# Reading q, k and V through one casting queue, and reordering the expert layer of a fused attention and mixture-of-experts kernel

## The chip, the cores and the metric

The kernel runs on one core of a Trainium2 chip. The core has five engines that work side by side: TensorE (PE: matrix products and transposes, with a separate row PEld for its weight loads), VectorE (DVE), ScalarE (ACT), GpSimd (POOL) and SyncE (SP). Sixteen DMA engines move data between DRAM and the core's memory. Three engines issue DMAs here: SP and ACT on hardware queues, POOL on a software queue (q0 in the profile) whose descriptors its own cores write, and which alone can cast f32 to bf16 on the way. The metric is the device time of one execution in microseconds (us); the median of several executions is compared.

## The reference

Block-causal attention over 8 batches, 8 heads, 576 positions and head size 64 is followed by a mixture of 8 experts on the 4,608 rows of 512 that attention yields. A row's expert is a hash of its token id.

```python
scores = scale * np.matmul(q, k.transpose(0, 1, 3, 2))     # (8, 8, 576, 576)
mask = (pos[:, None] // 64) >= (pos[None, :] // 64)
attn = softmax(np.where(mask, scores, -1e9))
x = np.matmul(attn, v).transpose(0, 2, 1, 3).reshape(4608, 512)
expert_idx = token_ids * 2654435761 % 8
for e in range(8):
    rows = expert_idx == e
    out[rows] = np.maximum(x[rows] @ w1[e], 0) @ w2[e]     # 512 -> 1024 -> 512
```

## The kernel before

The order of every engine's instructions is the order of the program text; each engine runs its own list strictly in that order and waits on semaphores where it needs another engine's result.

**Attention** is cut into 8 batches of four pairs (index g, 32 in all; r = g mod 4). A pair is two heads, one on partitions 0 to 63 and the other on 64 to 127. For each batch `load_qk` (L101) brings q and k as f32 on SP's queue, `cast_qk` (L109) casts them to bf16 on DVE, and `T_group` (L171) transposes 8 (or 4) blocks of 128x128 on PE into a PSUM tile `tp` and copies it into `qkT` with DVE (L184). Five T groups make a batch. `load_v` (L118) brings V as f32 in six DMAs on SP's queue, and `cast_v` (L152) casts it on POOL into the padded key tiles `vx` and `v4`, rows of 64 values and a 1 (so that the product also yields the row sums). There are two such sets.

For pair g the loop at L432 lays down, in this order: `S_chunk(g,0)` (scores of 512 queries, then an exponential on ACT, L220), one T group of the next batch (two when r = 3), `S_chunk(g,1)`, `PV(g-2,0)` (the product with V, L261), `S_chunk(g,2)` (with `S_rest` when r = 0), `PV(g-2,1)` and `norm(g-2)` on DVE (L271, L272). `scatter_x(b-1)` sends a finished batch's rows to a DRAM buffer sorted by expert, with five indirect DMAs on POOL's queue (L283). The slots come from `route`, some 40 small DVE instructions that are spread over the first pairs.

**The expert layer** begins once all rows are in DRAM. `load_x(e)` (L485) reads 640 rows of an expert on SP's queue, `turn_x(e)` (L505, L507) transposes them in groups of two 128-row tiles, through one PSUM buffer. `stage_a` (L520, 64 matmuls, relu on ACT) makes hT; `stage_b` (L535, 5 tiles of 8 matmuls) makes the output rows, which DVE copies (L540, four buffers `ysb`) and POOL scatters to DRAM (L542). `load_weights` (L398, L400) casts an expert's w1 and w2 through POOL's queue into three buffers. The main loop (L578) has, for each expert e: stage a, `turn_x(e+1)`, then `load_x(e+3)` and `load_weights(e+3)`, then stage b. Because `load_weights(e+3)` takes the buffers of expert e, POOL waits there until stage b of e has read w2, and the five scatters of e stand behind it on POOL.

Of the kernel before, what the change touches and what calls it, by code (L numbers as in the profile page):

```python
# [20 lines left out]
NT = 4  # L21
# [18 lines left out]
def kernel(  # L40
# [58 lines left out]
    qkf, qkb = {}, {}  # L99

    def load_qk(b, engs=(None, None)):  # L101
        for w, src in ((1, k), (0, q)):
            t = ld.tile([P, 2, JR, D], F32, name="qf" if w == 0 else "kf", tag="qf" if w == 0 else "kf")
            (engs[w] or nc.sync).dma_start(
                t[:].rearrange("p m j d -> p m (j d)"),
                src[b].rearrange("(m h) (g j) d -> (h g) m (j d)", m=2, j=JR))
            qkf[b, w] = t

    def cast_qk(b, w, j0=0, j1=JR, eng=None):  # L109
        if (b, w) not in qkb:  # L110
            qkb[b, w] = cst.tile([P, JR, 2, D], BF16, name="qb" if w == 0 else "kb",
                                 tag="qb" if w == 0 else "kb")
        o, i = qkb[b, w][:, j0:j1], qkf[b, w][:, :, j0:j1].rearrange("p m j d -> p j m d")
        (eng or nc.vector.tensor_copy)(o, i)

    vfs = {}

    def load_v(b):  # L118
        vf = lv.tile([P, 36, D], F32, name="vf", tag="vf")
        vm = vf[:, 0:32, :].rearrange("p (h i) d -> p h i d", h=H)  # L120
        for i in range(NT):
            nc.sync.dma_start(
                vm[:, :, i, :], v[b, :, 128 * i : 128 * i + 128, :].rearrange("h p d -> p h d"))
        for m in range(2):
            nc.sync.dma_start(
                vf[64 * m : 64 * m + 64, 32:36, :],
                v[b, 4 * m : 4 * m + 4, 512:576, :].rearrange("r s d -> s r d"))
        vfs[b] = vf

    vexts = []  # L130
    for z in range(2):
# [19 lines left out]

    def cast_v(b):  # L152
        vf = vfs.pop(b)
        vx, v4 = vexts[b % 2]
        nc.gpsimd.tensor_copy(  # L155
            vx[:, :, :, 0:D], vf[:, 0:32, :].rearrange("p (h i) d -> p h i d", h=H))
        for m in range(2):
            nc.gpsimd.tensor_copy(
                v4[64 * m : 64 * m + 64, :, m, 0:D], vf[64 * m : 64 * m + 64, 32:36, :])
# [6 lines left out]
        [(1, j) for j in range(16, 18)] + [(0, j) for j in range(16, 18)],  # L166
        [(1, j) for j in range(8, 16)],
        [(0, j) for j in range(8, 16)],
    )

    def T_group(b, n):  # L171
# [5 lines left out]
        for c, (w, j) in enumerate(items):  # L177
            nc.tensor.transpose(  # L178
                out=tp[:, c, :], in_=qkb[b, w][:, j].rearrange("p m d -> p (m d)"), identity=identbf[:])
        c = 0  # L180
        while c < len(items):
            w, j0 = items[c]
            n = sum(1 for x in items if x[0] == w)
            nc.vector.tensor_copy(  # L184
                qk[:, :, w, :].rearrange("p h (g j) -> p h g j", j=JR)[:, :, :, j0 : j0 + n],
                tp[:, c : c + n, :].rearrange("p j (h g) -> p h g j", h=NP))
            c += n
# [61 lines left out]
    def PV(g, m):  # L249
# [6 lines left out]
        vx, v4 = vexts[b % 2]  # L256
# [148 lines left out]
    load_qk(0, engs=(nc.scalar, None))  # L405
    load_v(0)
    load_qk(1)
    zx = const.tile([P, XW], BF16, name="zx")
    nc.gpsimd.memset(zx[:], 0.0)
    for e in range(E):  # L410
        nc.sync.dma_start(x_dram[(e + 1) * CAP - P : (e + 1) * CAP, :], zx[:])
    load_v(1)
# [11 lines left out]
    for n, (w, j0, j1) in enumerate(((1, 0, 8), (0, 0, 8), (1, 16, 18), (1, 8, 16), (0, 8, 16))):
        cast_qk(0, w, j0, j1)
        if n == 2:
            cast_qk(0, 0, 16, 18)
        T_group(0, n)
    cast_v(0)
    cast_qk(1, 1)  # L430
    cast_qk(1, 0)
    for g in range(NPAIRS + 2):  # L432
        b, r = divmod(g, NP)
        if g < NPAIRS:
            S_chunk(g, 0)
        if g + 1 < NPAIRS and b + 1 < B:
            T_group(b + 1, r)
            if r == 3:
                T_group(b + 1, 4)
# [13 lines left out]
        if r == 0 and b + 2 < B:  # L453
            load_qk(b + 2)
        if r == 1 and b + 2 < B:
            cast_qk(b + 2, 1)
        if r == 2 and b + 2 < B:
            cast_qk(b + 2, 0)
        if r == 1 and b >= 1:
            scatter_x(b - 1)  # L460
        if r == 2 and b + 1 < B:
            cast_v(b + 1)
            if b + 2 < B:
                load_v(b + 2)
        if g < NPAIRS:
            if b == 6 and r == 0:
                load_weights(0)
            if b == 7 and r == 0:
                load_weights(1)
            if b == 7 and r == 2:  # L470
                load_weights(2)
# [7 lines left out]
    psY = ffn_ctx.enter_context(tc.tile_pool(name="psY", bufs=3, space=PSUM))  # L479
    psX = ffn_ctx.enter_context(tc.tile_pool(name="psX", bufs=1, space=PSUM))  # L480
# [16 lines left out]
    def turn_x(e):  # L497
        xT = mx.tile([P, NKT, CAP], BF16, name="xT", tag="xT")
        xg = xgs[e]
        for g0 in range(0, G, 2):  # L500
            n = min(2, G - g0)
            tp = psX.tile([P, 2 * NKT, P], BF16, name="tx", tag="tx")
            for gg in range(n):
                for db in range(NKT):
                    nc.tensor.transpose(out=tp[:, gg * NKT + db, :],  # L505
                                        in_=xg[:, g0 + gg, db * P : (db + 1) * P], identity=identbf[:])
            nc.vector.tensor_copy(  # L507
                xT[:, :, g0 * P : (g0 + n) * P].rearrange("p d (g c) -> p g d c", g=n),
                tp[:, 0 : n * NKT, :].rearrange("p (g d) c -> p g d c", g=n))
        xTs[e] = xT  # L510
# [19 lines left out]
    def stage_b(e, hT):  # L530
        _, w2b = wtiles[e]
        for tt in range(G):
            yp = psY.tile([P, DM], F32, name="yp", tag="yp")
            for ft in range(NFT):
# [3 lines left out]
                )  # L538
            ysb = mo.tile([P, DM], F32, name="ysb", tag="ysb")
# [34 lines left out]
    for e in range(3):  # L574
        load_x(e)
    out_rows(0)
    turn_x(0)
# [178 lines left out]
```

## Time and profile before

| | |
|---|---|
| median of 3 runs | 376.84 us (372.2 to 377.64) |
| the profiled execution | 377.55 us; span 375.5 us from first to last instruction |
| busy share of the span | PE 74%, DVE 42%, ACT 39%, POOL 34% |
| mean granted TensorE clock | 0.89 of 2.4 GHz |
| DMA queues, share of 16 engines' time | q0 (POOL, software) 38.5%, 31.24 MB; q1 (SP) 31.6%, 33.86 MB; q10 (ACT) 0.9% |
| stretches (us from the span's start) | until the first score matmul 0 to 24.0; eight batches 24.0 to 136.5 (seven) and to 160.5; hand-over to the experts to 178.1; experts to 365.7; last scatters to 375.5 |

A row of the timeline is a start, a duration, the engine, the source line, the operation, output<-input, the shapes and a count; in brackets stands how long the engine had been idle and what ended that. DMA bytes are counted as written, so a cast to bf16 counts half of what it read.

### The profile page before, as it was taken

How to read it: one execution, taken by the hardware profiler on the slowest of the kernel's cores; microseconds unless marked ns; L12 is line 12 of the kernel's file. 1: busy time of each engine (PE TensorE's matmuls, PEld its weight loads, DVE VectorE, ACT ScalarE, POOL GpSimd, SP SyncE). 2: the span in 40 equal slices, each digit the busy share in tenths (PEclk: the TensorE clock that was granted, in tenths of full speed). 3: DMA queues.
4: the chain of work that ended last, by engine and by line, in shares of the span. 5: the costliest groups of instructions: out<-in, count | busy, mean ns of one | idle time of the engine just before them, and what ended most of it. 6: DMA issues, size and time to landing. Idle time of an engine off the chain costs nothing. (4 is left out here: it accounts for less than half of the span.)

```text
span 375.5 us, 6897 instructions
## 1 busy us (share of the span) xinstructions
PE 277.3 (74%) x2888; PEld 177.7 (47%) x2888; DVE 157.9 (42%) x278; ACT 144.8 (39%) x177; POOL 125.8 (34%) x155
## 2 busy tenths in 40 slices
PE   0358597897987867502989599598696895999990
PEld 0235465565665645402555446346254463464640
DVE  5679967877869533202031220220321312314230
ACT  1028497897887858100322304106014032050500
POOL 4303027547457645350003305104123151413241
PEclk9999898999989978555799979899699898999996
DMA  8999995979888788997266785778739756211121
GB/s 285 294 286 319 297 258 218 264 240 302 240 300 192 125 170 140 219 225 223 74 101 131 191 188 77 190 162 159 170 90 218 138 66 181 86 43 58 64 87 40
DMA packets 65971, 66.75 MB, mean 178 GB/s; under 512 B 39941, under 2 KB 54277, under 8 KB 65936
## 3 DMA queue, kind: packets, MB, share of 16 engines
q0 software_dynamic: 17536, 31.24, 38.5%
q1 hardware_dynamic: 48128, 33.86, 31.6%
q10 hardware_dynamic: 272, 1.18, 0.9%
q8 instruction: 23, 0.38, 0.4%
q14 instruction: 12, 0.10, 0.1%
HBM read 67.47 MB, written 16.61 MB: 224 GB/s over the span
## 5 line engine op out<-in xcount | busy, mean ns | idle before, releaser
L220 ACT ACTIVATE pt<-ps 128x1024 bf16<-128x1024 f32 x96 | 93.4, 1025 | 53.1 <-PE ps L203 39.8
L525 ACT ACTIVATE hT<-hp 128x640 bf16<-128x640 f32 x64 | 45.1, 704 | 158.5 <-PE hp L520 157.5
L535 PE MATMUL yp<-w2b,hT 128*128 128x512 bf16 x320 | 79.8, 414 | 0.0
L520 PE MATMUL hp<-xT,w1b 128*128 128x320 bf16 x512 | 73.7, 306 | 0.2 <-DVE xT L507 0.2
L540 DVE COPY ysb<-yp 128x512 f32<-128x512 f32 x40 | 27.7, 692 | 107.4 <-DMA out_dram<-ysb,perm 59.9
L542 POOL DMA_INDIRECT out_dram<-ysb,perm x40 | 40.0, 1000 | 69.7 <-DVE ysb L540 35.0
L520 PEld LDWEIGHTS <-w1b 128*128 128x128 bf16 x512 | 51.1, 100 | 22.6 <-issue 0.6
L283 POOL DMA_INDIRECT x_dram<-xs,slot_i x40 | 44.0, 1100 | 52.1 <-DVE xs L272 37.0
L194 PE MATMUL ps<-qkT 64*128 64x512 bf16 (+4 forms) x320 | 44.9, 328 | 16.8 <-DVE qkT L184 9.4
L535 PEld LDWEIGHTS <-hT 128*128 128x128 bf16 x320 | 33.5, 106 | 43.1 <-issue 12.6
L261 PE MATMUL O<-vx,pt 128*128 128x65 bf16 x896 | 44.3, 206 | 8.5 <-DVE xs L272 5.5
L184 DVE COPY qkT<-tp 128x1024 bf16<-128x1024 bf16 (+1 forms) x48 | 44.5, 950 | 9.0 <-PE tp L178 6.0
L505 PE MATMUL tx<-identbf,xg 128*128 128x128 bf16 x160 | 14.9, 240 | 41.7 <-DVE xT L507 26.9
L261 PEld LDWEIGHTS <-pt 128*128 128x128 bf16 x896 | 36.5, 105 | 14.2 <-DVE xs L272 4.4
L194 PEld LDWEIGHTS <-qkT 64*128 64x128 bf16 x320 | 18.3, 100 | 31.0 <-issue 12.1
L505 PEld LDWEIGHTS <-xg 128*128 128x128 bf16 x160 | 11.7, 107 | 44.5 <-issue 43.9
L507 DVE COPY xT<-tx 128x1024 bf16<-128x1024 bf16 (+1 forms) x24 | 14.4, 600 | 30.8 <-PE tx L505 30.8
L400 POOL DMA_DIRECT2D w2b<-in_moe_w_dram x8 | 7.6, 945 | 58.9 <-PE yp L535 58.9
L272 DVE TENSOR_TENSOR xs<-O,rsall 128x640 bf16<-128x640 f32 x32 | 26.4, 824 | 1.2
L203 PE MATMUL ps<-maskq,maskk 64*128 64x64 bf16 x256 | 25.0, 204 | 0.0
L155 POOL CAST vx<-vf 128x2048 bf16<-128x2048 f32 x8 | 15.2, 1902 | 21.4 <-DMA vf<-in_v_dram 21.4
L271 DVE RECIPROCAL rsall<-O 128x10 f32<-128x10 f32 x32 | 7.0, 218 | 34.3 <-PE O L264 23.0
(101 smaller groups left out, 160.5 us busy)
## 6 DMA issues: line engine op xcount, KB each, us to landing
kf<-in_k_dram SPq DMA_DIRECT2D x8, 1152.0 KB
vf<-in_v_dram SPq DMA_DIRECT2D x32, 256.0 KB
w1b<-in_moe_w_dram POOLq DMA_DIRECT2D x8, 1024.0 KB
w2b<-in_moe_w_dram POOLq DMA_DIRECT2D x8, 1024.0 KB
qf<-in_q_dram SPq DMA_DIRECT2D x7, 1152.0 KB
xg<-x_dram SPq DMA_DIRECT2D x8, 680.0 KB
qf<-in_q_dram ACTq DMA_DIRECT2D x1, 1152.0 KB
x_dram<-zx SPq DMA_DIRECT2D x8, 136.0 KB
```

The costliest lines, as they stand in the source:

```text
L184: nc.vector.tensor_copy(qk[:, :, w, :].rearrange("p h (g j) -> p h g j", j=JR)[:, :, :, j0 : j0 + n], tp[:, c : c + n, :].rearrange("p j ( ...
L194: nc.tensor.matmul(ps[:, m, o0 : o0 + n], lhsT=qk[rows, r, 1, 128 * i : 128 * i + 128], rhs=qk[rows, r, 0, q0 : q0 + n], start=True, stop= ...
L220: nc.scalar.activation(ptv[:, :, 512 * ch : 512 * ch + 512], ps[:], ACT.Exp, scale=SCALE)
L261: nc.tensor.matmul(dst, lhsT=pt[:, o0 : o0 + 128], rhs=vx[:, h, i, :], start=(i == 0), stop=(i == t))
L272: nc.vector.tensor_tensor(out=xss[b % 2][:, :, 0:DM].rearrange("p t (m r d) -> p m t r d", m=2, r=NP)[:, :, :, r, :], in0=Ov[:, :, :, 0:D] ...
L283: ins = nc.gpsimd.indirect_dma_start(out=x_dram[:, :], out_offset=bass.IndirectOffsetOnAxis(ap=slot_i[0:n, i, b : b + 1], axis=0), in_=xs[ ...
L505: nc.tensor.transpose(out=tp[:, gg * NKT + db, :], in_=xg[:, g0 + gg, db * P : (db + 1) * P], identity=identbf[:])
L520: nc.tensor.matmul(hp[:, t, 0:HC], lhsT=w1b[:, db, ft * P : (ft + 1) * P], rhs=xT[:, db, t * HC : (t + 1) * HC], start=(db == 0), stop=(db ...
L525: nc.scalar.activation(hT[:, ft, :].rearrange("p (t n) -> p t n", t=2), hp[:, :, 0:HC], ACT.Relu)
L535: nc.tensor.matmul(yp[:], lhsT=hT[:, ft, tt * P : (tt + 1) * P], rhs=w2b[:, ft, :], start=(ft == 0), stop=(ft == NFT - 1),)
L540: nc.vector.tensor_copy(ysb[:], yp[:])
L542: ins = nc.gpsimd.indirect_dma_start(out=out[:, :], out_offset=bass.IndirectOffsetOnAxis(ap=perm3[:, gg : gg + 1], axis=0), in_=ysb[:], in ...
```

## The change

It has five parts.

1. q, k and V are read by POOL's queue, which casts them on the way: `load_qk` writes bf16 `[P, 2, 18*64]` tiles in three buffers, `load_v` writes straight into three sets of `vx`/`v4`. The casts on DVE and POOL go, and so do the f32 tiles. Batch 0 of q and k comes in two halves. The constant fills (`set_fixed`) move from POOL to DVE.
2. The q and k tiles now keep the two head halves apart, so a block is transposed in two matmuls of 64 columns each, one per half (twice as many transposes).
3. The T groups of the next batch stand at other places: two at r = 0, two at r = 1, one at r = 2, none at r = 3. In batch 0 two of the five copies go to ACT.
4. In the expert layer `turn_x` works on one 128-row tile at a time, with two PSUM buffers, and tile tt of expert e+1 is turned inside stage b of e, behind tile tt's matmuls.
5. `load_x` and `load_weights` are issued two experts ahead, before stage a, and not three ahead, before stage b. Weights 0 and 1 are issued in attention, weights 2 after it.

```diff
-        for w, src in ((1, k), (0, q)):
-            t = ld.tile([P, 2, JR, D], F32, ...)
-            (engs[w] or nc.sync).dma_start(t[:].rearrange("p m j d -> p m (j d)"), src[b]...)
-        (eng or nc.vector.tensor_copy)(o, i)                      # cast_qk, DVE
+        src = (q, k)[w][b].rearrange("(m h) (g j) d -> (h g) m (j d)", m=2, j=JR)
+        nc.gpsimd.dma_start(qkb[b, w][:, :, j0 * D : j1 * D], src[:, :, j0 * D : j1 * D])
...
-            nc.sync.dma_start(
-                vm[:, :, i, :], v[b, :, 128 * i : 128 * i + 128, :].rearrange("h p d -> p h d"))
-        nc.gpsimd.tensor_copy(vx[:, :, :, 0:D], vf[:, 0:32, :]...)   # cast_v, POOL
+            nc.gpsimd.dma_start(
+                vx[:, :, i, 0:D], v[b, :, 128 * i : 128 * i + 128, :].rearrange("h p d -> p h d"))
...
-            nc.tensor.transpose(
-                out=tp[:, c, :], in_=qkb[b, w][:, j].rearrange("p m d -> p (m d)"), identity=identbf[:])
+            for m in range(2):
+                nc.tensor.transpose(
+                    out=tp[64 * m : 64 * m + 64, c, :], in_=qkb[b, w][:, m, j * D : (j + 1) * D],
+                    identity=identbf[:])
...
+        turns = ((0, 1), (2, 3), (4,), ())[r] if b + 1 < B else ()
...
+        if r == 2 and b + 2 < B:
+            load_v(b + 2)
+        if r == 3 and b + 3 < B:
+            for w in (1, 0):
+                load_qk(b + 3, w)
+        if g == 4 * 6 or g == 4 * 7 + 1:
+            load_weights(g // 4 - 6)
...
+            if e + 1 < E:
+                turn_x(e + 1, tt)          # in stage_b, behind tile tt's matmuls
...
     for e in range(E):
+        if e + 2 < E:
+            load_x(e + 2)
+            load_weights(e + 2)
         hT = stage_a(e)
         if e + 1 < E:
             out_rows(e + 1)
-            turn_x(e + 1)
-        if e + 3 < E:
-            load_x(e + 3)
-            load_weights(e + 3)
         stage_b(e, hT)
```

POOL at the start of the program, before (`vx` and `v` are the key tiles, `iota_e` the numbers that `route` needs on DVE, `vf` the f32 V):

```order
L84 IOTA jmp 128x128
L409 MEMSET zx 128x544
...
L150 MEMSET xs_122 128x5x32
L150 MEMSET xs_123 128x5x32
L310 IOTA iota_e 128x8
L155 CAST vx_113<-vf 128x32x64
```

The same place now. A wait on DMASW0 to DMASW7 is one for the landing of an earlier DMA of this queue: there are eight such semaphores, so a ninth DMA waits for the first to land.

```order
L84 IOTA jmp 128x128
L104 DMA kb<-in_k_dram 128x2x576
L104 DMA qb<-in_q_dram 128x2x576
...
L134 DMA v_108<-in_v_dram 64x4x64 [waits DMASW0_49]
L134 DMA v_108<-in_v_dram 64x4x64 [waits DMASW1_49,DVE_49]
L104 DMA kb<-in_k_dram 128x2x1152 [waits DMASW2_49]
L104 DMA qb<-in_q_dram 128x2x1152 [waits DMASW3_49]
L289 IOTA iota_e 128x8
L131 DMA vx_109<-in_v_dram 128x8x64 [waits DMASW4_49]
```

`iota_e` now stands behind twelve DMA issues, of which the last four wait for the landing of q and k of batch 0.

DVE in one batch of attention, before (`tp` to `qkT` are the T groups' copies, RECIPROCAL and TENSOR_TENSOR are `norm`):

```order
L114 CAST kb<-kf 128x2304
L184 COPY qkT<-tp 128x4x32x2 x2
L271 RECIPROCAL rsall<-O 128x10
L272 TENSOR_TENSOR xs_123<-O,rsall 128x2x5x64
L114 CAST qb<-qf 128x2304
L184 COPY qkT<-tp 128x4x32x8 x2
```

and now:

```order
L163 COPY qkT<-tp 128x4x32x8 x2
L250 RECIPROCAL rsall<-O 128x10
L251 TENSOR_TENSOR xs_118<-O,rsall 128x2x5x64
L163 COPY qkT<-tp 128x4x32x2 x2
L250 RECIPROCAL rsall<-O 128x10
L251 TENSOR_TENSOR xs_119<-O,rsall 128x2x5x64
```

The two casts are gone, and the last copies of a batch are the small ones of r = 2; before, two large copies stood at the end of r = 3, directly ahead of the next batch's first scores.

DVE in the expert layer, before (`prf`, `perm` are the output rows' numbers, `tx` to `xT` the turned rows, `yp` to `ysb` the results):

```order
L493 TENSOR_SCALAR prf<-xg 128x5
L494 TENSOR_TENSOR prf<-prf,pvalid 128x5
L495 TENSOR_SCALAR perm_73<-prf 128x5
L507 COPY xT<-tx 128x2x4x128 x2
L507 COPY xT<-tx 128x4x128
L540 COPY ysb<-yp 128x512 x5
```

and now:

```order
L465 TENSOR_SCALAR prf<-xg 128x5
L466 TENSOR_TENSOR prf<-prf,pvalid 128x5
L467 TENSOR_SCALAR perm_73<-prf 128x5
L476 COPY xT<-tx 128x4x128
L508 COPY ysb<-yp 128x512
```

The last two rows stand five times per expert: a copy of the next expert's rows now comes between two result copies, where before three copies stood in a block of their own behind the five result copies of the expert before.

## Rows read from the trace of the kernel before

**Rows 1.** Stretches of the program; columns are named in the first row.
```profile
core 0: us, PE busy (x) PEld busy (x) DVE busy (x) ACT busy (x) POOL busy (x), PEclk, DMA share, GB/s
24.00:44.20 20.20, 14.03 (x176) 8.98 (x175) 19.58 (x41) 12.60 (x14) 3.37 (x4) 1.00 1.05 278
...
89.80:104.50 14.70, 12.12 (x236) 9.08 (x237) 12.00 (x16) 12.11 (x14) 8.69 (x9) 1.00 0.91 261
...
119.80:136.50 16.70, 12.55 (x236) 9.29 (x237) 10.04 (x16) 11.33 (x14) 12.47 (x14) 0.99 0.80 136
136.50:160.50 24.00, 16.45 (x260) 12.42 (x259) 6.78 (x13) 13.17 (x15) 9.25 (x13) 0.64 0.89 178
160.50:178.10 17.60, 2.36 (x20) 2.06 (x21) 1.89 (x5) 0.00 (x0) 4.86 (x5) 0.50 0.91 228
178.10:201.50 23.40, 21.59 (x127) 12.41 (x125) 5.41 (x11) 5.63 (x8) 0.81 (x1) 0.87 0.45 105
201.50:227.70 26.20, 21.73 (x126) 12.42 (x125) 5.58 (x11) 5.63 (x8) 6.83 (x7) 0.87 0.71 151
...
328.00:348.30 20.30, 18.73 (x126) 11.34 (x125) 5.68 (x11) 5.63 (x8) 4.89 (x6) 1.00 0.16 59
348.30:365.70 17.40, 17.40 (x106) 10.08 (x104) 5.46 (x15) 5.64 (x8) 4.97 (x6) 1.00 0.18 66
365.70:375.50 9.80, 0.09 (x1) 0.00 (x0) 0.69 (x1) 0.00 (x0) 1.34 (x2) 0.63 0.11 39
```

**Rows 2.** Waits of PE in attention: total us, times, longest.
```profile
PE ps L194 <- DVE qkT L184: 9.4, 5, 2.6
```

**Rows 3.** The same view, expert layer.
```profile
DVE ysb L540 <- DMA out_dram<-ysb,perm: 59.9, 5, 12.1
POOL w2b L400 <- PE yp L535: 58.9, 5, 12.6
PE tx L505 <- DVE xT L507: 26.1, 15, 3.8
```

**Rows 4.** Timeline of PE in batch 4: score matmuls and T groups.
```profile
84.91 0.62 PE L178 MATMUL tp<-identbf,kb 128*128 128x128 bf16 x8
...
85.37 0.61 PE L178 MATMUL tp<-identbf,qb 128*128 128x128 bf16 x8
...
93.65 0.39 PE L194 MATMUL ps<-qkT 64*128 64x512 bf16 x2
...
96.45 0.39 PE L194 MATMUL ps<-qkT 64*128 64x512 bf16 x2
```

**Rows 5.** DMA queues (packets, MB, engines' time); 30-35, 36-38.5, 157-160, 162.5-165.5 us.
```profile
q1 hardware_dynamic: 449, 2.00, 100.6%
...
q1 hardware_dynamic: 1959, 0.51, 103.5%
...
q0 software_dynamic: 314, 0.64, 111.5%
...
q0 software_dynamic: 608, 0.62, 124.4%
```

**Rows 6.** Groups by line: issuing a DMA of 1,024 pieces on POOL.
```profile
L400 POOL DMA_DIRECT2D w2b<-in_moe_w_dram x8 | 7.6, 945 | 58.9 <-PE yp L535 58.9
```

**Rows 7.** Timeline of POOL and DVE in batch 4: scatter issues beside casts and copies.
```profile
100.83 1.35 DVE L114 CAST qb<-qf 128x2304 bf16<-128x2304 f32 x1
102.11 2.34 DVE L184 COPY qkT<-tp 128x1024 bf16<-128x1024 bf16 x2
...
101.33 1.69 POOL L283 DMA_INDIRECT x_dram<-xs,slot_i  x1 [0.30 <-issue]
103.32 0.96 POOL L283 DMA_INDIRECT x_dram<-xs,slot_i  x1 [0.30 <-issue]
```

**Rows 8.** Timeline of PE while weights 0 are read on q0.
```profile
133.89 0.27 PE L194 MATMUL ps<-qkT 64*128 64x192 bf16 x2 [0.95 <-issue]
...
135.32 0.54 PE L261 MATMUL O<-vx,pt 128*128 128x65 bf16 x12 [0.96 <-issue]
```

**Rows 9.** Timeline of the hand-over: rows read from DRAM, and their first use.
```profile
169.88 8.87 SPq L485 DMA_DIRECT2D xg<-x_dram  x4
...
174.18 1.01 PE L505 MATMUL tx<-identbf,xg 128*128 128x128 bf16 x8 [14.84 <-DMA xg<-x_dram]
```

**Rows 10.** Timeline of PE: turning expert 2's rows, between its two stages.
```profile
214.52 0.90 PE L505 MATMUL tx<-identbf,xg 128*128 128x128 bf16 x8 [3.69 <-DVE xT L507]
```

More of the change, by code (lines that the diff above doesn't have):

```diff
@@ L165, with T_group @@
         [(0, j) for j in range(0, 8)],
-        [(1, j) for j in range(16, 18)] + [(0, j) for j in range(16, 18)],
         [(1, j) for j in range(8, 16)],
         [(0, j) for j in range(8, 16)],
+        [(1, j) for j in range(16, 18)] + [(0, j) for j in range(16, 18)],
     )
-    def T_group(b, n):
+    def T_group(b, n, copy):
         if b not in qkTs:
@@ L420 @@
         nc.vector.memset(maskq[64 * m : 64 * m + 1, :], 1.0)
-    set_fixed()
     rgen = route()
     next(rgen)
[L424 to L431, printed above, removed]
+    T_group(0, 0, nc.vector.tensor_copy)
+    T_group(0, 1, nc.scalar.copy)
+    T_group(0, 2, nc.vector.tensor_copy)
+    T_group(0, 3, nc.scalar.copy)
+    T_group(0, 4, nc.vector.tensor_copy)
+    load_v(1)
+    for w in (1, 0):
+        load_qk(2, w)
     for g in range(NPAIRS + 2):
         b, r = divmod(g, NP)
+        turns = ((0, 1), (2, 3), (4,), ())[r] if b + 1 < B else ()
         if g < NPAIRS:
             S_chunk(g, 0)
[L436 to L439, printed above, removed]
+        for n in turns[0:1]:
+            T_group(b + 1, n, nc.vector.tensor_copy)
         if g < NPAIRS:
@@ L447 @@
                 S_rest(b)
+        for n in turns[1:2]:
+            T_group(b + 1, n, nc.vector.tensor_copy)
         if g >= 2:
@@ L452 @@
             next(rgen, None)
[L453 to L458, printed above, removed]
         if r == 1 and b >= 1:
             scatter_x(b - 1)
[L461 to L471, printed above, removed]
+        if r == 2 and b + 2 < B:
+            load_v(b + 2)
+        if r == 3 and b + 3 < B:
+            for w in (1, 0):
+                load_qk(b + 3, w)
+        if g == 4 * 6 or g == 4 * 7 + 1:
+            load_weights(g // 4 - 6)
     att_ctx.close()
@@ L478 @@
     psH = ffn_ctx.enter_context(tc.tile_pool(name="psH", bufs=2, space=PSUM))
[L479 to L480 removed]
+    psY = ffn_ctx.enter_context(tc.tile_pool(name="psY", bufs=2, space=PSUM))
+    psX = ffn_ctx.enter_context(tc.tile_pool(name="psX", bufs=2, space=PSUM))
     xgs, xTs = {}, {}
@@ L495, in out_rows, with turn_x @@
         nc.vector.tensor_single_scalar(perm3[:, e * G : (e + 1) * G], prf[:], float(N), op=ALU.add)
[L497 to L510, printed above, removed]
+    def turn_x(e, tt):
+        if e not in xTs:
+            xTs[e] = mx.tile([P, NKT, CAP], BF16, name="xT", tag="xT")
+        tp = psX.tile([P, NKT, P], BF16, name="tx", tag="tx")
+        for db in range(NKT):
+            nc.tensor.transpose(out=tp[:, db, :], in_=xgs[e][:, tt, db * P : (db + 1) * P],
+                                identity=identbf[:])
+        nc.vector.tensor_copy(xTs[e][:, :, tt * P : (tt + 1) * P], tp[:])
     def stage_a(e):
@@ L572, in sums_in_range @@
         nc.vector.tensor_single_scalar(ctl[:, 3:4], nov[:], float(E * G), op=ALU.add)
-    for e in range(3):
+    for e in range(2):
         load_x(e)
+    for tt in range(G):
+        turn_x(0, tt)
     out_rows(0)
-    turn_x(0)
     for e in range(E):
+        if e + 2 < E:
+            load_x(e + 2)
+            load_weights(e + 2)
         hT = stage_a(e)
```

70 lines of the change are left out of this document (26 added, 44 removed).

## The prediction, made before the changed kernel had run

> **What bounds the kernel now.** I read the busy times by stretch first [rows 1], since the shares of the whole span mix stages with different limits. In batch 0 DVE is busy 19.58 of 20.20 us: it sets that stage. In a steady batch (89.8 to 104.5) PE, DVE and ACT have 12 us each of 14.70: none is full, so the waits must say what is lost. They name PE waiting for the T groups' copies: 9.4 us in five waits, up to 2.6 us [rows 2]. Two large copies stand at the end of r = 3, ahead of the next batch's first scores. In the experts the last two rows show what PE needs: 17.40 us without any turning, 20.30 with turning and no weights being read; yet experts 0 and 1 take 23.40 and 26.20 at a clock of 0.87. The waits there [rows 3] form one chain. POOL waits 58.9 us in five waits for stage b before it issues w2; the result scatters stand behind it; DVE's fifth result copy waits for a free `ysb` (59.9 us, five times); the copies of turned rows stand behind that on DVE; and PE waits for those (26.1 us, 3.69 at expert 2 [rows 10]).
>
> Stretches of before: 24.0 start + 20.2 (batch 0) + 92.3 (six batches, 44.2 to 136.5, 15.4 each) + 24.0 (batch 7 and last pairs) + 17.6 (hand-over) + 187.6 (experts) + 9.8 (end) = 375.5. The run took 377.55: 2.05 outside the span, 0.7 over the median.
>
> **The change, part by part.**
>
> *Start: 24.0 to 21 (18 to 24).* The casts of q and k go from DVE and the reads come in halves. Against this, `iota_e`, which `route` on DVE needs, now stands behind twelve issues on POOL, four of which wait for landings; k and q of batch 0 take 512 packets x 178 ns / 16 = 5.7 us [rows 5], issue and landing some 11 in all, so I put the first T group at 13 us. The fills on DVE run while the first data is read, and cost nothing; without that cover they are inside the 24.
>
> *Batch 0: 20.2 to 19 (15 to 20).* DVE loses casts of 1.35 us [rows 7] and two copies, but keeps `route`. PE's 14.03 is the floor.
>
> *Six batches: 15.4 to 14.5 each, 87 in all.* (a) The T copies are finished at r = 2, so the wait at the batch's edge goes: 9.4 / 5 = 1.9 us [rows 2]. What is late next is nothing on DVE, which loses two casts of 1.35. (b) Twice as many transposes. Eight take 0.46 us, 57 ns each [rows 4]. A batch has 36 blocks: if the two halves of a block run beside each other this adds nothing, if one after the other 36 x 57 = 2.1 us. I take the middle, 1.0, for no row shows two such halves. A batch thus takes 15.4 - 1.9 + 1.0 = 14.5 (13.5 to 15.6). A pair with one T group took 2.80 us [rows 4]. (c) Covers. ACT 12.1 [rows 1]. POOL: eight issues at 0.945 us [rows 6] and five scatters at 0.96 + 0.30 [rows 7], 13.9: under 14.5, narrowly. DMA: q and k 5.7; a scatter of 0.63 MB at the 400 GB/s of the q1 stretch (2.00 MB in 5 us) 1.6; and V, 4,608 pieces of 128 bytes written from 256 read, a shape that no row shows. The rows: 256-byte pieces unchanged on q1 20.4 ns (2.5 us x 16 / 1,959), casting pieces on q0 79 ns for 1,024 bytes written and 153 for 2,048 [rows 5]. A line through these two gives 14 ns at 128 bytes, the lower end; 79 is the upper. I take 20.4, the nearest in size: 5.9 us. Together 13.2, hidden. At 79 ns V would take 22.8 (rival 1).
>
> POOL's issues could also be delayed by DVE. A scatter beside a DVE cast took 1.69 us, one wholly beside DVE's copies from PSUM 0.96 [rows 7]: the casts delay POOL, the copies don't, and the casts go. The Trainium skill ("SBUF — State Buffer", the box on the "DVE blocks DMA" trap) says that VectorE's fast modes, copies among them, hold the port it shares with GpSimd, so that descriptors aren't written; read as a rule for every DVE copy it would add some 5 us to POOL's batch, an estimate, and give about 360 us. By the rows the sum stays.
>
> *Batch 7 and last pairs: 24.0 to 23 (22 to 24).* No T groups in either kernel; half of one edge wait goes.
>
> *Hand-over: 17.6 to 19 (17.5 to 20.5).* PE waits 14.84 us for the first rows [rows 9]. Weights 2 are now issued behind the last scatters, so their read shares the engines with that of the rows. Weights take 512 x 153 / 16 + 1,024 x 79 / 16 = 10 us [rows 5]; I charge 1.4.
>
> *Experts: 187.6 to 150.3 (148 to 158).* `load_weights(e+2)` now takes the buffers of e-1, which are free when it is issued, so POOL doesn't wait and the scatters, the copies and PE behind it don't either. PE: 8 x 17.4 = 139.2; seven experts are turned with 20 transposes of 57 ns each, 1.14, 8.0 in all, since the copies now hide behind the next tile's matmuls (two PSUM buffers); the low clock of the first expert 23.4 - 20.3 = 3.1. The reads keep up: weights 10, results 1.31 MB and rows 0.66 MB at 400 GB/s 5, so 15 us of 18.5. The smaller turning groups and the earlier `load_x` cost nothing by themselves: stage a (64 of the 104 matmuls of the 17.40) and two whole experts cover the read. If they didn't, the wait would stand at PE's `tx`.
>
> *End: 9.8.* Same last scatters.
>
> Sum: 21 + 19 + 87 + 23 + 19 + 150.3 + 9.8 = 329.1, + 2.05 = 331.1; 330 against the median. Its own range, with the ends above not all falling together: 318 to 345.
>
> **The rivals.**
>
> *1, slower: V's small pieces make q0 the bound.* All of q, k and V now go through one queue, in order. If V takes V us per batch, the queue runs without pause from about 14 us through seven batches of 5.7 + 1.6 + V, and batch 7 follows with 23: attention ends at 88.5 + 7V, where my sum has 150. At 79 ns per piece V = 22.8, attention ends at 248, and the kernel takes 330 + 98 = 428. It decides from V = 8.8 (31 ns); the whole gain is gone at V = 15.3 (53 ns), and the kernel is 2% slower from 57 ns. For: per byte written, the two casting rows cost twice what q and k cost on q1, and no row has casting pieces this small. Against: the cost of casting pieces falls in proportion to their size, and the 256-byte row shows no floor above 20 ns. The Trainium skill ("DMA: Bandwidth & Descriptors", Specifications) says that pieces under 512 bytes lose the line rate and are written by read-modify-write, which speaks against this change. The 256-byte pieces of the trace agree by half: they carry 12.5 bytes per ns where 4,608-byte ones carry 25.9. Chance 0.18: 0.05 within 2%, 0.13 slower.
>
> *2: q0's traffic slows every engine.* While weights 0 are read (some 10 us), the batch takes 16.70 us and not 14.70 [rows 1], and PE stands for 0.95 and 0.96 us with nothing to wait for [rows 8]. If all of q0's reads do this, 13.2 us of them per batch cost 2.0 x 13.2 / 10 = 2.6 us, 21 in eight batches: 351, and 361 if the weights of five experts do it as well. Against: the pauses are two, and could be something that happens once. Chance 0.17, 345 to 370.
>
> *3: turning isn't hidden.* If experts keep the 20.30 of the row, 7 x 20.3 + 17.4 + 3.1 = 162.6: 342. This is inside my own range. Likewise, if POOL still waited before w2 the experts would stay at 187 and the time be 367; the order of the issues excludes it.
>
> **How the numbers follow.** The forecast has 0.60, rival 1 0.18, rival 2 0.17, and 0.05 is for less than 318 (halves side by side, no start penalty, no low clock). About 2%, 369.3 to 384.4, is what a measurement can tell from no change. Faster: 0.60 + 0.17 + 0.05, less 0.01 for the top of rival 2, 0.81. Same: 0.05 + 0.01. Slower: 0.13. The range leaves out the 0.05 below and 0.15 of rival 1: 318 to 374. The forecast's own range is 318 to 345.
>
> **What would show it.** Experts: PE at about 18.5 us per stage, clock 1.0, no wait of POOL for `yp` at w2, and none of DVE for `ysb` over 2 us. Attention: score matmuls of successive batches 14.5 us apart, no wait for `qkT` at the batch's edge, q0's V pieces near 20 ns. Wrong would be: PE's T groups waiting for the DMA of `kb`, or `O` for that of `vx`, at a DMA share near 1 (rival 1); pauses of PE by issue about every 5 us (rival 2); a T group with 16 transposes in 0.92 us and not 0.46 (the serial end); a first T group well after 13 us.

## The result, and the profile after

The changed kernel takes 337.62 us (median of four runs, 336.15 to 339.49) against 375.42 for the kernel before (372.2 to 377.64): a ratio of 0.900, with a 95% interval of 0.891 to 0.909. It is faster by 38 us, the forecast was 330. The profiled execution took 336.78 us with a span of 335.0. On another chip the same kernel took 362.31 us, which the experiments come to.

The stretches of the span of the changed kernel, in the columns of [rows 1]:

```profile
0.00:21.60 21.60, 4.63 (x79) 4.08 (x79) 9.86 (x44) 3.33 (x3) 14.10 (x25) 1.00 1.19 166
21.60:41.10 19.50, 14.28 (x212) 9.75 (x214) 13.36 (x36) 11.78 (x14) 8.95 (x16) 0.65 1.87 176
41.10:55.05 13.95, 12.20 (x276) 9.05 (x274) 9.37 (x14) 12.18 (x15) 2.88 (x3) 1.00 0.31 69
...
69.00:86.20 17.20, 13.74 (x277) 10.12 (x276) 9.55 (x14) 12.39 (x15) 11.46 (x15) 0.90 1.22 174
86.20:100.10 13.90, 12.13 (x273) 9.00 (x272) 9.37 (x14) 12.13 (x15) 11.38 (x14) 1.00 1.17 140
100.10:116.60 16.50, 13.72 (x277) 9.93 (x276) 9.51 (x14) 12.38 (x15) 11.48 (x15) 0.90 1.24 176
...
130.55:150.40 19.85, 14.37 (x263) 11.16 (x260) 6.27 (x12) 12.59 (x15) 8.88 (x12) 0.80 0.83 167
150.40:175.10 24.70, 2.49 (x22) 2.08 (x22) 2.65 (x6) 0.00 (x0) 6.67 (x7) 0.50 1.10 217
175.10:196.10 21.00, 20.76 (x127) 12.08 (x126) 5.44 (x15) 5.62 (x8) 3.57 (x4) 0.89 0.32 113
...
215.00:234.00 19.00, 18.62 (x128) 11.29 (x126) 5.52 (x13) 5.62 (x8) 6.81 (x8) 1.00 0.97 214
...
328.00:335.00 7.00, 0.01 (x1) 0.00 (x0) 0.69 (x1) 0.00 (x0) 1.26 (x2) 0.65 0.15 55
```

Each stretch beside the forecast. In [rows 1] the hand-over begins at the end of the last `norm` (160.5); the table has it so for both kernels, from 151.5 in the changed one. The lines above cut at the end of PE's last product, 1.1 us earlier:

| stretch | before | forecast | after |
|---|---|---|---|
| start | 24.0 | 21 | 21.6 |
| batch 0 | 20.2 | 19 | 19.5 |
| six batches | 92.3 | 87 | 89.5 |
| batch 7 and last pairs | 24.0 | 23 | 21.0 |
| hand-over | 17.6 | 19 | 23.6 |
| experts | 187.6 | 150.3 | 152.9 |
| end | 9.8 | 9.8 | 7.0 |
| span | 375.5 | 329.1 | 335.0 |

The experts gave 35 of the 40 us of the span. There the answer to [rows 3] is that the chain is gone: of the waits of that stretch, which name the waiting engine and line, the engine waited for, the total, the times and the longest, the view has no line of POOL for w2b and none of DVE for the landing of results, and PE waits 2.9 us in all:

```profile
POOL out_dram L510 <- DVE ysb L508: 82.2, 31, 10.2
...
DVE ysb L508 <- PE yp L501: 5.3, 5, 1.2
PE hp L486 <- DVE xT L476: 2.9, 8, 0.4
```

DVE now waits for PE, as it should where PE is the bound. Successive experts start 18.98 us apart at full clock.

In attention four of the six batches take 13.95 us, and the third and the fifth 17.15 and 16.45. In the third, PE stands twice for the tiles of q and k, which the timeline of PE shows (start, duration, instruction, and in brackets the idle time ahead and its end):

```profile
70.20 0.64 PE L156 MATMUL tp<-identbf,kb 128*64 128x128 bf16 x16 [0.77 <-DMA kb<-in_k_dram]
...
74.05 1.06 PE L156 MATMUL tp<-identbf,qb 128*64 128x128 bf16 x16 [1.37 <-DMA qb<-in_q_dram]
```

The 1.06 us where 0.64 is usual is the other half of that price: after the wait, the granted clock is at the lower of its two levels, 1.2 GHz (mean 0.90 in this batch). The lateness begins on POOL, one batch and a half earlier. Its timeline in the third and fourth batch, for the reads that the fifth waits for:

```profile
82.55 1.04 POOL L262 DMA_INDIRECT x_dram<-xs,slot_i  x1 [3.37 <-issue]
...
88.66 3.65 POOL L131 DMA_DIRECT2D vx<-in_v_dram  x4
...
93.48 0.79 POOL L104 DMA_DIRECT2D kb<-in_k_dram  x1
94.18 0.80 POOL L104 DMA_DIRECT2D qb<-in_q_dram  x1
```

By the order of the program the scatter waits for the last `norm` of the batch before (80.93 to 81.75 on DVE). Behind it stand five scatter issues (6.1 us), six of V (4.9), then q and k. The reads of q take a median of 10.2 us from issue to landing, and PE finds q missing at 104.49 [1.42 <-DMA qb]. In the hand-over PE waits for the first rows, as in [rows 9], but for 21.9 us and not 14.84:

```profile
161.52 14.70 SPq L457 DMA_DIRECT2D xg<-x_dram  x4
```

```profile
172.28 1.04 PE L474 MATMUL tx<-identbf,xg 128*128 128x128 bf16 x8 [21.88 <-DMA xg<-x_dram]
```

From the issue of the read to its use 10.8 us pass. Before, it was 4.3.

### The profile page after: what moved, and what is told of

It reads as the page before. It is cut to its first block, busy times and chain, and to the rows that moved or that the text cites. A ratio compares the mean times of both kernels' runs of the same rounds, so it can differ in the third digit from the quotient of the medians.

```text
span 335.0 us, 7408 instructions
## 1 busy us (share of the span) xinstructions
PE 261.9 (78%) x3176; PEld 173.1 (52%) x3176; DVE 133.8 (40%) x292; ACT 146.1 (44%) x179; POOL 147.8 (44%) x181
## 5 line engine op out<-in xcount | busy, mean ns | idle before, releaser
L199 ACT ACTIVATE pt<-ps 128x1024 bf16<-128x1024 f32 x96 | 92.7, 1023 | 25.9 <-PE ps L182 18.1
L501 PE MATMUL yp<-w2b,hT 128*128 128x512 bf16 x320 | 74.9, 379 | 0.0
L476 DVE COPY xT<-tx 128x512 bf16<-128x512 bf16 x40 | 16.9, 425 | 116.7 <-PE tx L474 116.7
L262 POOL DMA_INDIRECT x_dram<-xs,slot_i x40 | 39.1, 979 | 45.0 <-issue 38.4
L163 DVE COPY qkT<-tp 128x1024 bf16<-128x1024 bf16 (+1 forms) x46 | 42.5, 940 | 21.9 <-PE tp L156 21.9
L240 PE MATMUL O<-vx,pt 128*128 128x65 bf16 x896 | 42.6, 202 | 10.8 <-DVE xs L251 10.7
L501 PEld LDWEIGHTS <-hT 128*128 128x128 bf16 x320 | 30.1, 98 | 29.8
L173 PE MATMUL ps<-qkT 64*128 64x512 bf16 (+4 forms) x320 | 42.0, 315 | 3.8 <-ACT pt L199 2.7
L240 PEld LDWEIGHTS <-pt 128*128 128x128 bf16 x896 | 34.7, 103 | 17.3 <-DVE xs L251 13.5
L474 PE MATMUL tx<-identbf,xg 128*128 128x128 bf16 x160 | 16.2, 230 | 22.2 <-DMA xg<-x_dram 21.9
L131 POOL DMA_DIRECT2D vx<-in_v_dram x32 | 28.9, 921 | 7.6 <-DMA vx<-in_v_dram 4.2
L173 PEld LDWEIGHTS <-qkT 64*128 64x128 bf16 x320 | 17.1, 97 | 17.2 <-issue 6.0
L156 PE MATMUL tp<-identbf,kb 128*64 128x128 bf16 x288 | 14.8, 249 | 6.3 <-DVE qkT L163 5.3
## 6 DMA issues: line engine op xcount, KB each, us to landing
x_dram<-zx SPq DMA_DIRECT2D x8, 136.0 KB, 7.4
```

The source lines that it names most:

```text
L131: nc.gpsimd.dma_start(vx[:, :, i, 0:D], v[b, :, 128 * i : 128 * i + 128, :].rearrange("h p d -> p h d"))
L163: copy(qk[:, :, w, :].rearrange("p h (g j) -> p h g j", j=JR)[:, :, :, j0 : j0 + n], tp[:, c : c + n, :].rearrange("p j (h g) -> p h g j", ...
L173: nc.tensor.matmul(ps[:, m, o0 : o0 + n], lhsT=qk[rows, r, 1, 128 * i : 128 * i + 128], rhs=qk[rows, r, 0, q0 : q0 + n], start=True, stop= ...
L199: nc.scalar.activation(ptv[:, :, 512 * ch : 512 * ch + 512], ps[:], ACT.Exp, scale=SCALE)
L240: nc.tensor.matmul(dst, lhsT=pt[:, o0 : o0 + 128], rhs=vx[:, h, i, :], start=(i == 0), stop=(i == t))
L262: ins = nc.gpsimd.indirect_dma_start(out=x_dram[:, :], out_offset=bass.IndirectOffsetOnAxis(ap=slot_i[0:n, i, b : b + 1], axis=0), in_=xs[ ...
```

## Experiments

Runs of one group ran on one chip, beside runs of the kernel before on that chip. The first group and half_scatter had chip 5 (before: 376.33 and 376.38 us), the second group chip 14 (381.74), the rest of the third chip 7 (382.34). That matters, as will be seen.

### First group: the two delays, and the two parts of the expert layer

**qk_early**: the reads of q and k ahead of the scatter and of V.

```diff
+        if r == (0 if b else 3) and b + 3 < B:
+            for w in (1, 0):
+                load_qk(b + 3, w)
         if r == 1 and b >= 1:
             scatter_x(b - 1)
-        if r == 3 and b + 3 < B:
-            for w in (1, 0):
-                load_qk(b + 3, w)
```

> The changed kernel with one move: from batch 1 on, load_qk(b+3) is issued at r = 0, ahead of scatter_x(b-1) and load_v(b+2), and not behind them at r = 3. In the changed kernel batches 3 and 5 took 17.15 and 16.45 us and the four others 13.95; in both PE waits for kb and qb. Theory A (a loop of latency: norm at 10.35 us into batch b, then 6.1 us of scatter issues, 6 of V issues and 1.5 of q and k on POOL, then some 10 us until q and k land, against 27.9 us until batch b+2 wants them): the reads are now issued 12 us earlier, all six batches take 13.95 and the span falls by 3.1 + 2.5 = 5.6, from 335.0 to about 329.5. Theory B (the DMA engines cannot move a batch of q, k, V and scattered rows in less than some 15.3 us, the mean of batches 3 to 6): the late batches stay late, or others become late, and the span stays within 1.5 of 335.0.

331.63 us, ratio 0.880 (0.874 to 0.886), span 329.9. Theory A: all six batches take 13.96 to 14.00, two of them here, with the columns of [rows 1]:

```profile
69.13:83.10 13.97, 12.20 (x276) 9.05 (x274) 9.36 (x14) 12.20 (x15) 10.83 (x15) 1.00 1.30 164
...
97.07:111.03 13.96, 12.19 (x275) 9.05 (x272) 9.36 (x14) 12.19 (x15) 10.66 (x13) 1.00 1.12 153
```

The same bytes are moved, so it was the place in the queue and not what the DMA engines can carry.

**w2_late**: weights 2 out of the hand-over.

```diff
         if e + 2 < E:
             load_x(e + 2)
-            load_weights(e + 2)
+            if e > 0:
+                load_weights(e + 2)
...
             out_writes.append(ins)          # in stage_b
+            if e == 0 and tt == 0:
+                load_weights(2)
```

> The changed kernel with one move: the weights of expert 2 are issued behind the first result scatter of expert 0, and not behind the last scatters of attention. In the changed kernel PE waits 21.9 us for the first rows; their read is issued at 161.5 and is in at 172.3, 10.8 us, where before it took 4.3. Theory A (weights 2 are read at the same time and slow it): the read takes about 4.5 us again, the hand-over 18 and not 24.7, and the span falls by 6 to 6.5, to about 329. Theory B (the read is slow for another reason, such as the descriptors of the last scatters or two experts' rows at once): the hand-over stays at 23 to 25 and the span within 1 of 335.0.

329.27 us, ratio 0.873 (0.866 to 0.879), span 329.8. Theory A: the rows are read in 4.4 us, and the hand-over takes 17.1 from the end of the last `norm`, where the changed kernel took 23.6.

```profile
162.88 28.66 SPq L457 DMA_DIRECT2D xg<-x_dram  x5
```

```profile
167.24 1.03 PE L474 MATMUL tx<-identbf,xg 128*128 128x128 bf16 x8 [15.41 <-DMA xg<-x_dram]
```

The span fell by 5.2, not 6.5, because the two late batches were later here (17.6 and 17.2). The profiled execution took 331.67 us, one of the two slowest of six.

**issue_old**: without part 5 of the change.

```diff
-        if e + 2 < E:
-            load_x(e + 2)
-            load_weights(e + 2)
         hT = stage_a(e)
...
+        if e + 3 < E:
+            load_x(e + 3)
+            load_weights(e + 3)
         stage_b(e, hT)
```

> The changed kernel without its part 5: load_x(e+3) and load_weights(e+3) are issued behind stage a of e, as before; turn_x stays between the tiles of stage b. Theory A (the chain from POOL's wait for w2b over the scatters and the fifth result copy to PE needs part 5 to go): POOL waits for stage b again, and the experts take 24 to 26 us each while weights are loaded: five times 5 to 7 us more, span 360 to 370. Theory B (with part 4 alone the turned rows are copied before the fifth result copy, so nothing that PE needs next stands behind it): POOL and DVE wait as before, but PE doesn't; experts stay near 19 us and the span within 5 of 335.

343.87 us, ratio 0.910 (0.903 to 0.918), span 343.4, experts 157.84. Theory B: POOL and DVE wait as before, yet PE hardly does.

```profile
POOL w2b L379 <- PE tx L474: 32.8, 5, 8.8
DVE ysb L508 <- DMA out_dram<-ysb,perm: 54.4, 5, 11.2
```

DVE's copy of a result waits 11.2 us, nearly as long as in [rows 3], and PE pays 4.5 us for it in all (five waits, of 0.2 to 1.25 us), since the next expert's rows are turned already. That the span rose by 8.4 and not by under 5 is 4.9 from the experts and 3.5 from the stretches ahead of them, which the edit doesn't touch.

**turn_old**: without part 4 (turning in groups between the stages, one PSUM buffer; the results `yp` have three again, as before, and not two).

```diff
         if e + 1 < E:
             out_rows(e + 1)
+            turn_x(e + 1)
...
-            if e + 1 < E:
-                turn_x(e + 1, tt)
```

> The changed kernel without its part 4: turn_x works in groups of two tiles between stage a and stage b, through one PSUM buffer, as before; the loads stay two experts ahead. Theory A (part 5 alone removes POOL's wait and with it the chain): each of seven experts costs what the last expert with turning cost before, 20.30 us, against 18.98 now: 7 x 1.3 = 9 us more, span 344. Theory B (the turning must stand inside stage b for the copies to be in time): DVE's copies of turned rows still stand behind result copies that wait for scatters, the experts take 23 us or more, span over 360.

346.76 us, ratio 0.918 (0.911 to 0.925), span 348.6, experts 162.5. Theory A: 20.33 us per expert, where before the one without weights took 20.30 [rows 1], 1.35 more than now. Of the span's rise of 13.6, 9.6 are the experts' and 3.9 lie ahead of them, as in issue_old. Twice per expert PE waits for a copy, 0.78 us each:

```profile
212.16 0.61 PE L477 MATMUL tx<-identbf,xg 128*128 128x128 bf16 x8 [0.78 <-DVE xT L479]
213.55 0.38 PE L477 MATMUL tx<-identbf,xg 128*128 128x128 bf16 x4 [0.78 <-DVE xT L479]
```

### Second group: four more edits, on a chip that does something else

**both**: the edits of qk_early and w2_late together.

> The changed kernel with both moves of the first two runs: q and k of batch b+3 are issued ahead of the scatter at r = 0, weights 2 behind the first result scatter of expert 0. If the two delays are separate, as told so far (5.1 and 6.5 us of the span), the span is 335.0 - 5.1 - 6.5 = 323.4, with six batches of 13.95 and a hand-over of 18. If the one only fills time that the other had left free, about 329.

**both_spread**: that, and

```diff
-        turns = ((0, 1), (2, 3), (4,), ())[r] if b + 1 < B else ()
+        turns = ((0,), (1,), (2, 4), (3,))[r] if b + 1 < B else ()
```

> As the run with both moves, and the T groups stand (0), (1), (2, 4), (3) at r = 0 to 3, and not (0, 1), (2, 3), (4), none. A pair took 3.91 us with two T groups, 2.81 with none (set by ACT), and before 2.80 with one. Theory A (a pair's second T group is what costs, since the first hides under ACT): a batch takes about 3.3 + 2.85 + 3.4 + 2.9 = 12.5, but POOL's 13.1 us of issues per batch come next: 13.1, 0.85 less than 13.95, span 5 lower than with both moves alone. Theory B (the wait at the batch's edge comes back, since the copy of group 3 ends late at r = 3): up to 1.8 more at the edge, 13.9 to 14.5, span the same or up to 3 higher.

**both_t_old**: as both, with `((0,), (1,), (2,), (3, 4))[r]` and the small T group third.

> As the run with both moves, with part 3 of the change undone: T groups in the old order (the small one third) and at the old places, (0), (1), (2), (3, 4). The prediction took 1.9 us per batch for the wait at the batch's edge that part 3 removes. Theory A (that wait is what part 3 brings): the six batches take 13.95 + 1.9 = 15.8, span 11 to 13 higher than with both moves. Theory B (part 3 only moves the cost: pairs with two T groups at r = 0 and 1 take 3.9 and not 2.8): 3.4 + 2.85 + 2.85 + 5.2 = 14.3, span 2 to 4 higher.

**ffn_old**: the changed kernel with the edits of issue_old and turn_old together.

> The changed kernel without its parts 4 and 5: attention as changed, the expert layer in the old order (turning in groups between the stages, loads three experts ahead behind stage a). Each part alone had kept most of the gain (experts 158 without part 5, 162 without part 4, 153 with both, 188 before). Theory A (either part breaks the chain that reaches PE, so only without both it comes back): experts about 186 to 190, span 335 + 35 = 370. Theory B (a good part of the experts' 188 came from somewhere else, such as the attention part's state at the hand-over): experts about 153 + 5 + 9.6 = 168, span 350.

| run | median us | ratio (95%) | span | seven batch starts from batch 1 on, us |
|---|---|---|---|---|
| both | 359.32 | 0.941 (0.937 to 0.944) | 358.4 | 41.0, 56.1, 78.4, 97.5, 116.1, 134.4, 153.4 |
| both_spread | 351.21 | 0.921 (0.917 to 0.924) | 349.6 | 38.3, 55.3, 74.1, 92.6, 110.5, 129.3, 147.2 |
| both_t_old | 358.30 | 0.939 (0.937 to 0.942) | 355.5 | 39.2, 56.6, 76.3, 96.4, 115.7, 134.0, 153.2 |
| ffn_old | 400.73 | 1.051 (1.045 to 1.058) | 398.9 | 41.7, 56.8, 78.4, 98.5, 117.2, 136.0, 154.8 |

None of the totals answers its question, because from batch 2 on a batch takes 18 to 22 us in all four. The stretches that lie apart from this do answer. In both, PE waits 14.0 us for the first rows, so the second edit holds. In ffn_old the experts take 187.03 us against 187.6 before (and 152.6 in both, on the same chip), and the chain of [rows 3] is back with the same sums. Parts 4 and 5 each keep most of the chain's cost from PE, and without both it is all there: theory A.

```profile
DVE ysb L512 <- DMA out_dram<-ysb,perm: 59.4, 5, 12.2
POOL w2b L379 <- PE yp L507: 58.6, 5, 12.6
```

What the places of the T groups are worth without the disturbance stays open. With it, both_spread is 9 us of the span ahead of both, and the old places 3. Batch 0, in which POOL issues no scatter, takes 16.2 us in both_spread and 16.1 in both_t_old against 19.1 in both; in batch 1 they take 1.9 and 2.3 more than both.

### Third and last group: the disturbance

**after_again** is the changed kernel, **before_again** the kernel before, both unchanged; **both_spread_again** is the kernel both_spread.

> The changed kernel itself, once more. In the last four runs, on another chip than the runs before them, every batch of attention from the second on took 18 to 20 us and not 14, with pauses of PE, ACT and DVE of about 1 us each while POOL issues scatters; the first four runs and the first profile of the changed kernel show none. Theory A (the pauses belong to that chip, or to what it does at that time, and meet every kernel whose q, k and V go through POOL's queue): on a chip without them the span is 335 and the ratio to before 0.90; on a chip with them the six batches take some 18.5 each, span 360 to 370, ratio 0.95 to 0.97. Theory B (the pauses came from the edits, which q and k ahead of the scatter and the old expert order have in common): the span is 335 and the ratio 0.90 on any chip.

> The kernel before itself, for a profile on the same chip as the run above. Its first profile shows pauses of PE for which nothing is waited (0.95 and 0.96 us) beside one scatter only, at 129.6 to 135.3 us; six other scatters run without. Theory A (pauses need POOL's scatter issues and a chip that has them; before has as many scatters): on a chip with pauses they stand beside most scatters, and the batches take 17 or more. Theory B (they need q0's casting reads in flight as well, which before has only while weights are read): at most one or two scatters of before have them on any chip, span 372 to 380.

> The kernel with both moves and the T groups at (0), (1), (2, 4), (3), once more, beside the changed kernel on one chip. Without pauses: both moves give 335.0 - 5.1 - 6.5 = 323.4, and the T groups, if a pair's second one is what costs, batches of 13.1 to 13.95 (POOL's issues come next at 13.1), span 318 to 323. With pauses as in the last four runs: span 350, and 10 to 18 less than the changed kernel beside it.

The changed kernel took 362.31 us on chip 7, ratio 0.952 (0.944 to 0.959), span 360.4; the kernel before, in one run, 377.78; both_spread 348.85, ratio 0.918 (0.909 to 0.926). So the change is faster by 10% on one chip and by 5% on another: theory A of after_again. Batches in the changed kernel there, with the columns of [rows 1]:

```profile
42.28:57.14 14.86, 12.43 (x276) 9.22 (x274) 9.38 (x14) 11.96 (x14) 3.48 (x4) 1.00 0.22 54
57.14:77.23 20.09, 14.97 (x274) 10.74 (x274) 9.37 (x14) 12.51 (x14) 12.70 (x16) 0.87 0.94 132
77.23:95.58 18.35, 14.42 (x274) 10.40 (x273) 9.38 (x14) 12.52 (x14) 11.29 (x15) 0.86 1.05 131
...
113.74:132.74 19.00, 15.63 (x275) 11.31 (x273) 9.37 (x14) 12.52 (x14) 11.50 (x15) 0.77 0.95 127
```

ACT and DVE do the same work as on the first chip; only PE's busy time is up, with its clock down. The pauses begin while POOL issues a set of five scatters and go on to about 1 us behind it. One set runs from 71.31 to 77.43. The timelines of POOL, DVE, ACT and PE there:

```profile
71.31 1.05 POOL L262 DMA_INDIRECT x_dram<-xs,slot_i  x1 [5.87 <-issue]
...
76.53 0.90 POOL L262 DMA_INDIRECT x_dram<-xs,slot_i  x1 [0.30 <-DMA x_dram<-xs,slot_i]
...
73.41 0.22 DVE L250 RECIPROCAL rsall<-O 128x10 f32<-128x10 f32 x1 [2.23 <-PE ps L173]
...
74.18 1.02 ACT L199 ACTIVATE pt<-ps 128x1024 bf16<-128x1024 f32 x1 [1.45 <-PE ps L173]
...
71.99 0.19 PE L243 MATMUL O<-v,pt 128*128 128x65 bf16 x1
...
72.99 0.21 PE L173 MATMUL ps<-qkT 64*128 64x64 bf16 x2
74.57 0.62 PE L240 MATMUL O<-vx,pt 128*128 128x65 bf16 x14 [1.37 <-PE ps L173]
...
78.41 0.25 PE L182 MATMUL ps<-maskq,maskk 64*128 64x64 bf16 x2 [0.58 <-issue]
```

DVE's reciprocal needs the product that PE ended at 72.2, and starts at 73.41. ACT's exponential needs scores that PE ended at 73.2, and starts at 74.18. Each hand-over between engines comes about 1 us late, PE itself stands where it waits for nothing shown (up to 78.41, behind the last scatter), and after that its clock is low. The experts of the same run are as fast as on chip 5, though POOL issues 40 scatters in them too, and q0 casts weights. The first line has the columns of [rows 1], the second is the group of POOL's issues there:

```profile
200.50:353.40 152.90, 149.98 (x975) 89.84 (x973) 44.37 (x109) 45.12 (x64) 47.64 (x49) 0.98 0.68 158
...
L510 POOL DMA_INDIRECT out_dram<-ysb,perm x40 | 40.0, 1001 | 120.1 <-DVE ysb L508 82.4
```

So POOL's issue of indirect DMAs on such a chip does not delay PE by itself. What attention has that the experts have not, no run separates.

Of the kernel before on this chip the batches take 14.5, 15.3, 16.9, 14.5, 14.7 and 17.6: some of its scatters have pauses (0.2 to 0.5 us at 71.9, 75.3, 87.4, 88.4, 135.0 and 136.5), most have not. Its median lies 6 us above that on chip 5; the profiled execution, the fastest of seven, 1.4. Its expectation was half right (theory B in the span, 375.8, but three disturbed sets of scatters and not two).

**half_scatter**: as both, with the scatters of batches 1, 3 and 5 put off to the end of attention.

```diff
-    xss = [fix.tile([P, 5, XW], BF16, name=f"xs{z}") for z in range(2)]
+    xss = [fix.tile([P, 5, XW], BF16, name=f"xs{z}") for z in range(5)]
...
-        if r == 1 and b >= 1:
+        if r == 1 and b >= 1 and b - 1 not in (1, 3, 5):
             scatter_x(b - 1)
...
+    for b in (1, 3, 5):
+        scatter_x(b)
```

> The kernel with both moves, and the scatters of batches 1, 3 and 5 put off until the last scatter of attention has been issued (three more buffers of rows). So POOL issues scatters in batches 1, 3, 5 and 7, and none in 2, 4 and 6, in one run on one chip. On a chip with pauses: if POOL's scatter issues are needed for them, batches 2, 4 and 6 take 13.95 and batches 3, 5 and 7 some 18; if q0's casting reads alone make them, all take 18 to 19. On a chip without pauses all six take 13.95. The three scatters at the end cost 3 x 6.4 = 19 us of the hand-over in either case: span 335.0 - 5.1 - 6.5 + 19 = 342 without pauses, some 355 with pauses in half of the batches, 370 with them in all.

340.36 us, ratio 0.907 (0.903 to 0.911), span 338.6, on chip 5 again: all six batches 13.94 to 13.97, as for a chip without pauses. It could not tell what makes the pauses. It does show that a batch is no faster with a scatter less on POOL's queue, so that queue does not set the 13.95. PE does: in the batch at 41.1 it is busy for 12.2 us and waits 1.3 for `norm` and 0.4 for ACT.

## Why the prediction came out as it did

The sum was 329.1 against 335.0, right in kind and in its largest term. Point by point:

- **Start, 21 against 21.6, and batch 0, 19 against 19.5: near in number.** The first T group stood at 15.6 us and not at 13, behind `route`, which waited for the `iota_e` that POOL ran at 13.45. Batch 0 ran at a mean granted clock of 0.65 (1.00 before [rows 1]), which the sum did not have; that it came out near is in part luck.
- **Experts, 150.3 against 152.9: right, by the named mechanism.** The stated chain is what cost 35 us (ffn_old brings it back). What I had not seen is that either part nearly suffices: with part 4 alone POOL and DVE still wait 33 and 54 us and it costs PE 4.5. Short in the sum is the start of each stage a, where PE waits 0.38 us for the last turned tile, which no stage b tile follows to hide: 2.9 us in eight waits. Against it, the low clock of the first expert cost 2.0 and not 3.1.
- **Hand-over, 19 against 23.6: the mechanism right, the term mis-sized.** The step "I charge 1.4" for weights 2 beside the read of the first rows should have been 6.5 (10.8 against 4.3 us). w2_late shows it.
- **Six batches, 87 against 89.5: errors that nearly cancel, so the nearness is luck.** The steady batch is 13.95 and not 14.5, and by other terms than mine. The 15.4 that I began with is a mean over batches at a lower clock and the one with the pauses of [rows 8]; the two at full clock took 14.6 and 14.7. The wait at the edge went, as stated (9.4 to 0.9 us in attention). The 1.0 for twice as many transposes was not spent: the two halves of a block run side by side. Sixteen halves take 0.57 us until PE's next work, eight whole ones took 0.55, as the timelines of PE show, before and after:

```profile
90.12 0.62 PE L178 MATMUL tp<-identbf,kb 128*128 128x128 bf16 x8
90.67 0.36 PE L194 MATMUL ps<-qkT 64*128 64x448 bf16 x2
...
41.45 0.64 PE L156 MATMUL tp<-identbf,kb 128*64 128x128 bf16 x16
42.02 0.36 PE L173 MATMUL ps<-qkT 64*128 64x448 bf16 x2
```

The step "What is late next is nothing on DVE" failed: two T copies at r = 0 and at r = 1 now stand ahead of `norm`, and PE waits for its result before it reuses `O`, 1.3 us per steady batch where it was 0.2. The waits of PE in attention, before and after:

```profile
PE O L261 <- DVE xs L272: 5.5, 9, 2.9
...
PE O L240 <- DVE xs L251: 10.7, 20, 1.2
```

Thus 14.65 - 1.8 + 0.1 + 1.1 = 14.05. On top of the steady batches the two late ones took 5.7 us, PE's waits for q and k and the low clock behind them. There the step that failed is the covers: POOL's 13.9 and DMA's 13.2 us were each held against a batch's time, and being less they counted as hidden. But the reads of q and k stand behind a scatter that waits for `norm`, so what counts is the way from `norm` to the landing, some 22 us, and where in the batch it begins. I had named what is queued on POOL and not added it up along the queue. qk_early shows it.
- **Batch 7, 23 against 21.0; the end, 9.8 against 7.0.** The work is the same in both kernels. In batch 7 the granted clock is 0.80 where it was 0.64 [rows 1]; before, this batch came right after the pauses of [rows 8], which after doesn't have. I had carried the low clock over; that the pauses made it is argued, not tested. The last scatter lands 6.0 us after its issue and not 8.7; why, no run tells.
- **V's pieces, 20.4 ns taken: right, even high.** From 92.0 to 94.5 us 2,632 of them pass on q0, 2.5 x 16 / 2,632 = 15.2 ns each. Rival 1 fell. One sign that I had named for it did come, T groups waiting for `kb` at a DMA share near 1 (1.22 in the third batch); in qk_early the share is 1.30 there and nothing waits, so it was not the engines' rate. (Attention's end in that rival adds up to 88.1 + 7V, not 88.5; nothing hangs on the 0.4.)

```profile
q0 software_dynamic: 2632, 0.33, 208.6%
```

The Trainium skill ("DMA: Bandwidth & Descriptors", Specifications) puts pieces under 512 bytes below the line rate. The trace agrees in direction: 16.8 bytes read per ns here, 25.9 in the large pieces of [rows 5]. It shows no price that would stop a batch of 13.95.
- **Rival 2, chance 0.17, 345 to 370: its effect came, on two of the three chips.** The first profile shows none of it: the batch at 41.1 with POOL nearly idle and that at 86.2 with q0 busy take 13.95 and 13.90. On chips 14 and 7 the batches from the second on take 18 to 22, and on chip 7 the kernel takes 362. But I had tied it to q0's casting reads, and the pauses stand from within a set of scatters to about 1 us behind it. [Rows 8] fit that: in that run a set was issued from 128.22 to 134.31, while the weights were read. I read the pauses as due to the weights; which of the two it was, that run does not tell.
- **DVE beside POOL's issues: by the rows.** The 40 scatter issues in attention take 0.98 us each on average. The rule of the Trainium skill ("SBUF — State Buffer", the box on the "DVE blocks DMA" trap), read as one for every copy, would have made them longer; with the casts gone, the trace shows no such delay. The box itself names fp32 copies within SBUF, and the copies left here come from PSUM, so the trace does not speak against it.

What stays open: why the engines are delayed around POOL's scatters on two of the three chips of the experiments. No group had one kernel of this layout with the pauses and one without, so no edit can be named. The kernel before has as many scatters in attention and loses far less, and the experts have as many and lose nothing, so more than the scatter is needed. Whether both edits together give the 323 that the two single runs add up to was not measured on a chip without pauses; the best measured there is w2_late, at 0.873. In half_scatter, which has both, no batch is late and the first rows are read in 4.2 us, so neither edit undoes the other.

## What to carry to other kernels

Where work moves to one in-order queue, add up the way along the queue from the last thing that it waits for to the landing, and hold that against when the data is wanted; a busy time under the stage's time says nothing of it. When a chain of waits passes through several engines, look for each place where it can be cut: here two, and either was nearly enough. A batch that comes out near the sum can still be made of other terms: hold each term against the trace, not the total alone. A read that hides behind other reads is charged by what it does to those that someone waits for, at the time when it runs.

## What was not expected of the hardware

The same program took 337 us on one chip and 362 on another, where the kernel before differed by 6. The difference lies in attention alone, in hand-overs between engines that came some 1 us late during and just behind POOL's sets of indirect DMAs (0.98 us each, unchanged); the experts, with 40 such DMAs of their own, took 152.9 us on both chips. And two half transposes that write different partition halves run side by side: sixteen took 0.64 us from the first start to the last end, eight whole ones 0.62.
